# Splitting three rows of a weight load by 117 and 11 partitions, and giving SyncE's load credits once

## The chip, the cores and the metric

The kernel runs on one core of a Trainium2 chip. The metric is the device time of one execution in microseconds (us). Where two kernels are compared by a ratio, it is the mean time of one kernel's fast runs over the mean time of the other's fast runs of the same rounds, so it is not quite the ratio of the medians that are quoted beside it.

## The reference, cut to what matters

One decode step of grouped-query attention for two sequences over a cache of 32,768 positions, times a small gated MLP:

```python
B, Sq, D = 2, 1, 512
Hq, Hkv, Sk, Dh = 32, 8, 32768, 128          # bfloat16
# k_cache, v_cache: [B, Hkv, Sk, Dh]; wo: [Hq * Dh, D]
scores = einsum("bhqd,bhkd->bhqk", q, k) * (Dh ** -0.5)
o = einsum("bhqk,bhkd->bhqd", softmax(scores), v)
s = o.reshape(B, Sq, Hq * Dh) @ wo           # wo comes last
g = silu(mlp(xn))
return x + s * g
```

Nearly all of the work is to read the two caches once: 16 pairs (sequence, head) with 8 MB of K and 8 MB of V each. wo has 4 MB.

## The kernel before

SyncE issues every large load. A K or V load of one pair is one DMA of 128 partitions with 64 KB each; the consumers count its two halves on two semaphores, so SyncE adds 16 to the second semaphore itself. wo is stored as two halves of 128 partitions x 16 rows of 1 KB. It is loaded last, in seven pieces that get smaller, and each piece has a semaphore on which TensorE starts its products.

```python
WO_PARTS = [(0, 0, 8), (0, 8, 16), (1, 0, 8), (1, 8, 12), (1, 12, 14), (1, 14, 15), (1, 15, 16)]

def load(cache, dst, sems, m):
    if m < last:
        sp.dma_start(out=dst, in_=row_view(cache, *groups[m])).then_inc(sems[0], 16)
        sp.sem_inc(sems[1], 16)
    else:
        for c in range(NPART):
            load_half(cache, dst, sems, m, c)
# ...
for m in range(1, NG):
    sp.wait_ge(p_k, m)
    load_k(m)
    sp.wait_ge(p_o, m)
    load_v(m)
wos = A_wo.rearrange("(g p r) d -> p g (r d)", p=128, r=RS)
for i, (g, r0, r1) in enumerate(WO_PARTS):
    w = slice(r0 * D, r1 * D)
    d_wo[i].after(sp.dma_start(out=wo3[:, g, w], in_=wos[:, g, w]), 16)
# ...
def product(i):                              # TensorE
    g, r0, r1 = WO_PARTS[i]
    wait(pe, (d_wo[i], 16))
    # four matmuls for each row
```

The softmax here doesn't subtract the row's maximum and nothing guards it: scores larger than these inputs give would overflow.

## Time and profile before

| | before |
|---|---|
| time, median of 3 runs | 654.95 us (654.88 to 655.34) |
| profiled span | 654.2 us |
| data queue's share of 16 DMA engines | 99.2% |
| first and last of the 16 landings of the last wo load | 649.74, 651.47 us |

From the profile page of the kernel before: the span in 40 slices (DMA in tenths, then GB/s), and the table of DMA queues (packets, MB, share of 16 engines).

```profile
DMA  8999999999999999999999999999999999999997
GB/s 368 442 439 448 442 413 429 445 445 429 417 445 445 441 401 445 445 437 405 445 445 445 409 437 445 445 433 409 445 445 445 397 445 445 445 425 417 437 429 293
...
q1 hardware_dynamic: 6492, 280.50, 99.2%
q8 instruction: 2, 0.03, 0.0%
q14 instruction: 2, 0.02, 0.0%
```

The DMA engines are almost never idle (99.2%), so the kernel is as fast as its loads. What can still differ is the end: the last load is done when the slowest of 16 engines is done. The chain of waits of the kernel before (start, length, what) says the same: one DMA piece up to 651.47 us, then only a few small steps.

```profile
614.34 0.34 SPq L451
614.68 0.05 issue
614.73 36.74 DMA kbuf<-in_A_wo_dram
651.47 0.04 issue
651.52 0.26 PE bank L614 x4
651.78 0.02 issue
651.80 0.30 DVE sg L638
```

The trace's semaphore records give the 16 landings of each load, read here as one for each engine. Of the last wo load:

```
649.74 649.75 649.76 649.77 649.81 649.82 649.83 649.85 649.89 649.99 650.10 650.12 650.22 650.38   650.97   651.47
```

The last two are called the stragglers here. A third engine (650.38) is half a us late.

### The profile page before, as it was taken

Reading aid. Unit: us, or ns where it says so; the run is one execution under the profiler, and the core shown is the slowest. Engines: PE = TensorE matmul, PEld = TensorE weight load, DVE = VectorE, ACT = ScalarE, POOL = GpSimd, SP = SyncE. Lnnn points to the kernel's source line nnn. Section 1 sums busy time; section 2 is a strip of 40 time slices with the busy share of each in tenths; the row PEclk is TensorE's granted clock in tenths of the full one; section 3 lists DMA queues with packets and bytes.
Section 4 is the critical chain, followed back from the end, with each engine's and each line's share of the span. In section 5 each row is a group of like instructions: output and inputs, shape, how many; then the busy total and the mean of one; then the engine's idle time right before and its main releaser. Section 6 shows DMA issues by size and latency. Waiting matters only on the chain. (4 is left out here: it accounts for less than half of the span.)

```text
span 654.2 us, 6541 instructions
## 1 busy us (share of the span) xinstructions
PE 390.2 (60%) x2406; PEld 156.8 (24%) x2438; DVE 345.7 (53%) x412; ACT 76.6 (12%) x184; POOL 7.7 (1%) x29
## 2 busy tenths in 40 slices
PE   0648285582838648293773829367283945828785
PEld 0222132230313212131231213123121322312322
DVE  4257092653909356291844719174480926539570
ACT  1320102010010200101020010201001020010100
POOL 3100000000000000000000000000000000000000
PEclk9769788696978868698786978878697896869798
DMA  8999999999999999999999999999999999999997
GB/s 368 442 439 448 442 413 429 445 445 429 417 445 445 441 401 445 445 437 405 445 445 445 409 437 445 445 433 409 445 445 445 397 445 445 445 425 417 437 429 293
DMA packets 6508, 280.56 MB, mean 429 GB/s; under 512 B 736, under 2 KB 1000, under 8 KB 1256
## 3 DMA queue, kind: packets, MB, share of 16 engines
q1 hardware_dynamic: 6492, 280.50, 99.2%
q8 instruction: 2, 0.03, 0.0%
q14 instruction: 2, 0.02, 0.0%
q10 hardware_dynamic: 12, 0.01, 0.0%
HBM read 280.50 MB, written 0.00 MB: 429 GB/s over the span
## 5 line engine op out<-in xcount | busy, mean ns | idle before, releaser
L562 PE MATMUL bank<-T,z 128*128 128x512 bf16 x992 | 271.6, 418 | 187.2 <-PEq L46 181.7
L489 DVE STREAM_TRANSPOSE T<-kbuf 128x1024 int32<-128x1024 int32 x256 | 290.5, 1206 | 127.2 <-DVEq L46 127.2
L562 PEld LDWEIGHTS bank<-T,z 128*128 128x128 bf16 x1024 | 96.0, 103 | 350.2 <-issue 274.4
L579 PE MATMUL bank<-vbuf,pt 128*16 128x512 bf16 x1024 | 75.6, 461 | 2.5 <-PEq L46 2.5
L466 ACT ACTIVATE ep<-bank 128x512 bf16<-128x512 f32 x32 | 19.1, 597 | 436.1 <-ACTq L46 436.1
L510 DVE RECIPROCAL rec<-bank 128x1 f32<-128x1 f32 (+1 forms) x17 | 2.9, 169 | 122.7 <-DVEq L46 122.7
L579 PEld LDWEIGHTS bank<-vbuf,pt 128*16 128x16 bf16 x1024 | 28.0, 104 | 41.9 <-issue 25.1
L498 DVE STREAM_TRANSPOSE pt<-ep 128x512 bf16<-128x512 bf16 x32 | 22.7, 708 | 22.0 <-DVEq L46 22.0
L544 PE MATMUL bank<-ob,sel_o 128*128 128x128 f32 x136 | 20.6, 298 | 16.4 <-PEq L46 16.4
L572 PE MATMUL bank<-ones_f,sm 128*128 128x1 f32 x32 | 6.6, 277 | 31.3 <-PEq L46 31.3
L544 PEld LDWEIGHTS bank<-ob,sel_o 128*128 128x128 f32 x136 | 17.7, 204 | 21.8 <-issue 21.8
L470 ACT COPY ob<-bank 128x512 f32<-128x512 f32 x16 | 9.4, 586 | 105.7 <-ACTq L46 105.7
L459 ACT ACT_TABLE_LOAD x16 | 20.5, 1283 | 0.3
L572 PEld LDWEIGHTS bank<-ones_f,sm 128*128 128x128 f32 x32 | 5.8, 225 | 32.2 <-issue 32.2
L459 ACT COPY z<-qr 32x16 bf16 x64 | 12.9, 201 | 0.7
L428 PE MATMUL bank<-vbuf,h_bf 128*32 128x512 bf16 x14 | 5.3, 565 | 5.7 <-DVE h_bf L425 5.7
L539 PE MATMUL bank<-ident 128*1 128x1 bf16 x64 | 8.4, 165 | 0.0
L305 PE MATMUL bank<-ident,xn_bf 17*128 17x17 bf16 x4 | 0.3, 179 | 13.4 <-POOL x L296 13.4
L539 PEld LDWEIGHTS bank<-ident 128*1 128x1 bf16 x64 | 4.0, 82 | 16.2 <-issue 14.4
L518 DVE TENSOR_REDUCE oA<-xm 128x128 f32 x16 | 5.9, 366 | 3.8 <-DVEq L46 3.8
L512 DVE SCALAR_TENSOR_TENSOR xm<-bank,rec,mask 128x128 f32<-128x128 f32 (+1 forms) x17 | 6.0, 351 | 2.5 <-DVEq L46 0.2
L466 ACT ACTIVATION_READ_ACCUMULATOR ep<-bank 128x1 f32 x32 | 6.4, 199 | 0.2
(75 smaller groups left out, 55.4 us busy)
## 6 DMA issues: line engine op xcount, KB each, us to landing
vbuf<-in_A_v_cache_dram SPq DMA_DIRECT2D x4, 4096.0 KB, 29.6
kbuf<-in_A_k_cache_dram SPq DMA_DIRECT2D x2, 4096.0 KB, 22.9
kbuf<-in_A_wq_dram SPq DMA_DIRECT2D x1, 4096.0 KB, 12.5
vbuf<-in_B_w_dram SPq DMA_DIRECT2D x2, 1792.0 KB, 17.4
kbuf<-in_A_wo_dram SPq DMA_DIRECT2D x3, 1024.0 KB, 34.4
kbuf<-in_A_wo_dram SPq DMA_DIRECT2D x1, 512.0 KB, 37.1
kbuf<-in_A_wo_dram SPq DMA_DIRECT2D x1, 256.0 KB, 37.3
kbuf<-in_A_wo_dram SPq DMA_DIRECT2D x2, 128.0 KB, 36.8
```

Source lines behind the costliest of these rows:

```text
L459: i = act.copy(out=z[32 * j:32 * j + 32, :, :, c:c + rep], in_=qr[32 * j:32 * j + 32, :, :, bass.ds(m * rep, rep)],)
L466: act.activation(out=eps_[i][:, :], in_=sc[i][:, :], func=ACT.Exp, scale=inv_sqrt_dh, accum_out=rss[i][:, :]).then_inc(s_e, 1)
L470: act.copy(out=ob[:, :], in_=o[:, :]).then_inc(s_ob, 1)
L489: dve.transpose(out=Ts[(NR * i + r) % T_BUFS][:, :].rearrange("p (b t k) -> p t b k", b=NB, t=RT), in_=kt[:, r * W:(r + 1) * W].rearrange( ...
L498: dve.transpose(out=pts[h][:, :, :].rearrange("p r (t h) -> p t r h", h=rep), in_=eps_[i][:, :].rearrange("p (t r h) -> p t r h", r=NR, h= ...
L512: dve.scalar_tensor_tensor(out=xm[p0:, :, :], in0=oT[p0:, :].rearrange("p (w r) -> p w r", w=WL), scalar=rec[p0:, 0:1], in1=mask[p0:, :].u ...
L518: dve.tensor_reduce(out=dst, in_=xm[p0:, :, :].rearrange("p w r -> p r w"), axis=AX.X, op=ALU.add).then_inc(s_r, 1)
L539: pe.matmul(mark_ps, lhsT=ident[:, 0:1], rhs=ident[:, 0:1], start=True, stop=True).then_inc(sem, 1)
L544: mm = pe.matmul(oT, lhsT=sel_o[:, t, :, :, :].rearrange("p j h w -> p (j h w)"), rhs=ob[:, t * Dh:(t + 1) * Dh], start=(t == 0), stop=(t ...
L562: mm = pe.matmul(sc[i][:, :], lhsT=z[:, nb, e, zc:zc + 128], rhs=Tb[:, nb, :, e], start=(r == 0 and nb == 0 and e == 0), stop=(r == NR - 1 ...
L572: pe.matmul(S, lhsT=sms[1][:, :], rhs=ones_f[:, 0:1], start=True, stop=True)
L579: mm = pe.matmul(o[32 * j:32 * j + VT * rep, :], lhsT=pts[h][:, r, a * VT * rep:(a + 1) * VT * rep], rhs=vt[:, u * VT:(u + 1) * VT, :].rea ...
```

## The change

The intent, as the diff suggests: let the high-numbered DMA engines carry less of wo, so that late engines end with the others. Rows 8 to 14 of the second half go as 3 + 3 instead of 4 + 2, and the first three rows are cut at partition 117 into a DMA on 13 engines (117 = 13 x 9) and one on 11. Besides, SyncE's increments for undivided loads are given once at the start.

```diff
-WO_PARTS = [(0, 0, 8), (0, 8, 16), (1, 0, 8), (1, 8, 12), (1, 12, 14), (1, 14, 15), (1, 15, 16)]
+WO_PARTS = [(0, 0, 8, ()), (0, 8, 16, ()), (1, 0, 8, ()), (1, 8, 11, (117,)), (1, 11, 14, ()), (1, 14, 15, ()), (1, 15, 16, ())]
@@ def load
             sp.dma_start(out=dst, in_=row_view(cache, *groups[m])).then_inc(sems[0], 16)
-            sp.sem_inc(sems[1], 16)
@@ after the first load of K
+    sp.sem_inc(s_k[1], 16 * last)
+    sp.sem_inc(s_v[1], 16 * (last - 1))
@@ loads of wo
-        d_wo[i].after(sp.dma_start(out=wo3[:, g, w], in_=wos[:, g, w]), 16)
+        for p0, p1 in zip((0,) + cuts, cuts + (128,)):
+            k_wo = d_wo[i].after(sp.dma_start(out=wo3[p0:p1, g, w], in_=wos[p0:p1, g, w]), 16)
+        l_wo.append(k_wo)
@@ early(i) and product(i): wait for the whole count
-        wait(pe, (d_wo[i], 16))
+        wait(pe, l_wo[i])
```

## The prediction

> **What bounds the kernel.** DMA. The table of DMA queues gives the one data queue 99.2% of 16 engines' span; the 40 slices show DMA at 9 tenths from start to end (280.5 MB, 429 GB/s), PE at 60%, DVE at 53%. The chain of waits ends in one 36.74 us piece, the last wo load (614.73 to 651.47), then 0.26 us of PE, 0.59 us of DVE and the store. So the time is set by when the slowest of the 16 DMA engines finishes its share of the last wo load.

> Every load so far gives every engine the same bytes, but they do not end together. The 16 landings of the last wo load (the trace's semaphore records): fourteen from 649.74 to 650.38, one at 650.97, one at 651.47. The lag is old: the first K load lands within 0.8 us, the next (78.9 us) has two stragglers 1.4 and 1.9 us behind the median, and it persists (1.1 and 1.6) because the queues never drain. In between, at 59.5 and 69.7 us, two 16 KB instruction packets take 0.93 and 0.96 us. [...] I read these as the stragglers' cause.

> **What the change does.** (a) wo rows 8 to 14 of the second half: 4+2 rows become 3+3, the first three loaded by 117 and by 11 partitions. [...] Then engines 13 to 15 carry nothing of those rows. Packets of 1, 2 and 4 KB follow each other after 42, 80 and 155 ns, so 3 KB needs about 118 ns (estimate). Per engine, rows 8 to 14: before 8x155 + 8x80 = 1.88 us; after, engines 0 to 10 18x118 = 2.12 (+0.25), 11 and 12 2.01 (+0.13), 13 to 15 0.94 (-0.94). Total bytes are unchanged. (b) 29 SyncE semaphore increments of 17 ns become two. SyncE waits 528 us for compute before loads while the DMA queue stays fed: 0.0 us. One more DMA issue (about 0.43 us) is off the path too: SyncE ends issuing wo at 622.9, 26 us before those bytes move. PE and DVE programs keep their order.

> **Worth.** If both stragglers are among engines 13 to 15, they end near 650.0 and 650.5, and the next engine (650.38 plus up to 0.25) near 650.6: -0.9 us. If only the slower one is, the other ends at about 651.2: -0.3. If neither: +0.25. I hold the first most likely, since the split was chosen so; the trace doesn't number its engines.

> **Prediction: 654.2 us, range 653.6 to 655.3.** Faster by over 2%: 0.01; within 2%: 0.98; slower: 0.01.

> **What would show it.** Right: the last load's landings span about 0.8 us instead of 1.73 and end near 650.6; the 117- and 11-partition loads show 13 and 11 landings; the first landings come 0.25 us later; both 16 KB instruction packets stay; groups of PE and DVE unchanged; loads issued at the same times. Wrong: a straggler still near 651.2 to 651.7.

> **What would make it wrong.** Stragglers with low numbers; instruction packets moving to other engines or times because SyncE's program is shorter; 3 KB packets costing more than interpolated; chip-to-chip differences as large as the effect.

The sum comes to 654.2 us, 0.75 us of gain between the -0.9 and the -0.3 us under "Worth". Its terms for the engines stand on three counts. The 13 and 11 engines were a supposition then. Equal shares, so 8 or 9 packets for each engine, are an estimate from 128 packets and 16 landings, or 117 and 13. That the engines without cut rows are numbers 13 to 15 was supposed. That the lag persists because the queues never drain is the reading of a data queue at 99.2%, not a separate measurement.

## More of the kernel before

A table by stretches of the kernel before, in us: busy time and instructions of each compute engine, granted clock, DMA share, GB/s. The last column is the one to read.

```profile
644.00:646.00 2.00, 2.00 (x17) 1.02 (x13) 0.00 (x0) 0.59 (x1) 0.00 (x0) 0.50 1.03 434
646.00:648.00 2.00, 1.29 (x14) 0.67 (x13) 0.80 (x3) 0.59 (x1) 0.00 (x0) 0.97 0.98 410
648.00:650.00 2.00, 0.84 (x40) 0.59 (x40) 0.09 (x1) 0.00 (x0) 0.00 (x0) 1.00 0.84 313
650.00:652.00 2.00, 1.16 (x32) 0.53 (x32) 0.20 (x1) 0.00 (x0) 0.00 (x0) 1.00 0.06 23
```

Nearly all engines are busy almost to 650 us (DMA share 0.84 in the last stretch before it); then two finish alone.

## The result

| | before | after |
|---|---|---|
| time, median of 6 runs | 654.96 us (654.88 to 655.34) | 656.31 us (655.87 to 656.47) |
| ratio of fast runs | | 1.0018, 95% interval 1.0005 to 1.0031 |
| profiled span | 654.2 us | 655.1 us |
| landings of the last wo load | 649.74 to 651.47 us | 649.70 to 652.38 us |

The change costs a little more than 1 us, where 0.75 us of gain had been predicted. By the 2% measure it is "same", and no two runs of the two kernels overlap.

The profile page of the kernel after, same lines:

```profile
DMA  9999999999999999999999999999999999999997
GB/s 369 440 440 446 441 432 412 444 444 440 404 444 440 444 436 408 444 444 444 408 436 440 448 436 404 448 440 444 432 412 444 444 440 404 444 440 418 436 428 262
...
q1 hardware_dynamic: 6500, 280.50, 99.2%
q8 instruction: 2, 0.03, 0.0%
...
q14 instruction: 1, 0.01, 0.0%
```

Up to the last slice the level is the same. The bytes and the share are the same too, but the last slice moves 262 GB/s instead of 293. A share of 99.2% doesn't tell an engine whose packet moves at full speed from one whose packet takes longer. (One 8 KB packet of q14, at 617.57 us before, is missing after. It doesn't decide the time: split_only below has it and is slow, uncut lacks it and is not.) The chain of waits of the kernel after:

```profile
611.83 39.93 DMA kbuf<-in_A_wo_dram
651.76 0.04 issue
651.81 0.93 PE bank L618 x19
652.74 0.02 issue
652.76 0.30 DVE sg L642
```

The chain still ends in the wo load. (The piece at L618 is longer only because it is followed back to the load before the last two, which landed at 651.76; the two after it landed at 652.11 and 652.38.) The stretches of the kernel after:

```profile
644.00:646.00 2.00, 1.58 (x22) 0.80 (x15) 0.00 (x0) 0.58 (x1) 0.00 (x0) 0.95 1.02 430
646.00:648.00 2.00, 1.13 (x14) 0.51 (x12) 0.89 (x3) 0.58 (x1) 0.00 (x0) 1.00 1.01 331
648.00:650.00 2.00, 0.30 (x24) 0.33 (x28) 0.00 (x0) 0.00 (x0) 0.00 (x0) 1.00 0.95 238
650.00:652.00 2.00, 1.24 (x56) 0.68 (x44) 0.00 (x0) 0.00 (x0) 0.00 (x0) 0.76 0.30 102
```

Here is the loss: from 646 to 650 us the engines are at least as busy as before (DMA share 1.01 and 0.95, before 0.98 and 0.84), but they move 331 and 238 GB/s where they moved 410 and 313. The records of single packets say which ones are slow (packets from 646.3 us on, durations in ns):

| packets | before | after |
|---|---|---|
| 8 KB | 38, all 309 | 20, mean 388, up to 604 |
| 3 KB | none | 256, mean 171, from 121 to 284 |
| 1 KB | 256, all 46 | 256, mean 58, up to 159 |

The first slow packet of the last stage starts at 646.97 us, about 0.6 us after the first 3 KB packet. Packets of all sizes are slow, the 8 KB ones of an ordinary 128-partition load too: something is shared. The extra time is 256 x (171.3 - 121) + 20 x (387.9 - 309) + 256 x (57.7 - 46) = 17.5 us, over 16 engines 1.1 us each. That is the size of the loss.

The table of DMA issues of the kernel after (KB each, time to landing) shows the two cut loads:

```profile
kbuf<-in_A_wo_dram SPq DMA_DIRECT2D x3, 1024.0 KB, 36.0
kbuf<-in_A_wo_dram SPq DMA_DIRECT2D x1, 384.0 KB, 39.9
kbuf<-in_A_wo_dram SPq DMA_DIRECT2D x1, 351.0 KB
kbuf<-in_A_wo_dram SPq DMA_DIRECT2D x2, 128.0 KB, 39.1
...
kbuf<-in_A_wo_dram SPq DMA_DIRECT2D x1, 33.0 KB
```

Their common semaphore has 26 updates: one at 611.56 and one at 611.96 us, just after each issue, and 24 from 648.66 us on. The 24 are 13 + 11 landings; the first two come 34 us before the first 3 KB packet starts (646.38 us), so they are none. In the load that follows, three engines land early, at 648.93, 649.22 and 649.34 us, the other thirteen from 650.01 on. If the cut load takes the first 13 engines in the numbering that the run labels gives below (supposed), these three are engines 13 to 15, which carried nothing of the cut rows. They lie within 0.4 us of each other, so none of them is a straggler.

### The profile page after: what moved, and what is told of

Read it like the earlier page. It is cut to its first block, busy times and chain, and to the rows that moved or that the text cites. A ratio compares the mean times of both kernels' runs of the same rounds, so it can differ in the third digit from the quotient of the medians.

```text
span 655.1 us, 6515 instructions
## 1 busy us (share of the span) xinstructions
PE 383.7 (59%) x2406; PEld 156.2 (24%) x2438; DVE 346.3 (53%) x412; ACT 76.5 (12%) x184; POOL 7.7 (1%) x29
## 3 DMA queue, kind: packets, MB, share of 16 engines
q1 hardware_dynamic: 6500, 280.50, 99.2%
## 5 line engine op out<-in xcount | busy, mean ns | idle before, releaser
L566 PEld LDWEIGHTS bank<-T,z 128*128 128x128 bf16 x1024 | 98.5, 104 | 353.1 <-issue 274.9
L583 PE MATMUL bank<-vbuf,pt 128*16 128x512 bf16 x1024 | 71.5, 441 | 4.6 <-PEq L46 4.6
L548 PE MATMUL bank<-ob,sel_o 128*128 128x128 f32 x136 | 19.2, 284 | 16.8 <-PEq L46 16.8
L548 PEld LDWEIGHTS bank<-ob,sel_o 128*128 128x128 f32 x136 | 16.5, 191 | 21.8 <-issue 21.8
## 6 DMA issues: line engine op xcount, KB each, us to landing
vbuf<-in_B_w_dram SPq DMA_DIRECT2D x2, 1792.0 KB, 17.4
```

The source lines that it names most:

```text
L548: mm = pe.matmul(oT, lhsT=sel_o[:, t, :, :, :].rearrange("p j h w -> p (j h w)"), rhs=ob[:, t * Dh:(t + 1) * Dh], start=(t == 0), stop=(t ...
L566: mm = pe.matmul(sc[i][:, :], lhsT=z[:, nb, e, zc:zc + 128], rhs=Tb[:, nb, :, e], start=(r == 0 and nb == 0 and e == 0), stop=(r == NR - 1 ...
L583: mm = pe.matmul(o[32 * j:32 * j + VT * rep, :], lhsT=pts[h][:, r, a * VT * rep:(a + 1) * VT * rep], rhs=vt[:, u * VT:(u + 1) * VT, :].rea ...
```

## The experiments

Three theories were set against each other.

- C, collision: the loads by 117 and 11 partitions send several DMA engines to the same part of SBUF at once, and they slow each other and their neighbours.
- P, packets: packets of 3 KB cost more than 1, 2 and 4 KB ones suggest.
- S, SyncE: its shorter program moves load issues or instruction packets.

Theory C rested on a supposed map of partitions to ports. What of it these runs show comes from ports3 below: two engines that write partitions 0 and 1, or 0 and 32, move 25.5 and 28.2 GB/s together; at 0 and 4, or 0 and 64, they move 47.9 and 47.4. Which partitions of a load one engine writes no trace shows; that it takes neighbours (nine of 117) is supposed.

Because profiles of one kernel differ by some tenths of a us in when wo begins, the table below counts from the median landing of the first wo load to the last landing of the last one ("tail").

| run | what differs from before | median us | ratio to before, 95% interval | tail us | 3 KB packets, mean ns |
|---|---|---|---|---|---|
| before (profile above) | | | | 9.10 | none |
| after (profile above) | all | 656.31 | 1.0018 (1.0005 to 1.0031) | 10.34 | 171 |
| credits_only | SyncE's credits | 655.09 | 0.9999 (0.9982 to 1.0015) | 8.85 | none |
| split_only | wo pieces and cut | 656.25 | 1.0017 (1.0000 to 1.0034) | 10.23 | 174 |
| uncut | all, without the cut | 655.22 | 1.0000 (0.9983 to 1.0016) | 9.15 | 121 (every one) |
| cut_126 | cut at 126 | 656.51 | 1.0018 (1.0001 to 1.0035) | 10.43 | 164 |
| cut_121 | cut at 121 | 656.77 | 1.0024 (1.0007 to 1.0041) | 10.51 | 190 |

The first three experiments ran on one chip with the same runs of before (median 655.07), the last two with others (median 655.14).

### credits_only

```diff
     if m < last:
         sp.dma_start(out=dst, in_=row_view(cache, *groups[m])).then_inc(sems[0], 16)
-        sp.sem_inc(sems[1], 16)
...
+    sp.sem_inc(s_k[1], 16 * last)
+    sp.sem_inc(s_v[1], 16 * (last - 1))
```

> Only the semaphore increments of SyncE are changed; wo is loaded as before. Theory C (the loads by 117 and 11 partitions make DMA engines collide): ratio to before 1.000, within 0.0005, about 655.0 us, DMA throughput near 420 GB/s from 647.0 to 648.5 us as before. Theory P (packets of 3 KB cost more): the same 1.000. Theory S (SyncE's shorter program moved instruction packets or load issues): 1.002, about 656.3 us, as the whole change.

655.09 against 655.07 us; every packet of the last stage at full speed (309, 159, 84 and 46 ns for 8, 4, 2 and 1 KB, as before). The credits make no difference that these runs can see, and theory S is out as the cause of the loss.

### split_only

```diff
-WO_PARTS = [... (1, 8, 12), (1, 12, 14), ...]
+WO_PARTS = [... (1, 8, 11, (117,)), (1, 11, 14, ()), ...]
 # with the increments of SyncE left where they were
```

> Only the wo pieces are changed; SyncE increments as before. Theories C and P: 1.002, about 656.3 us, 3 KB packets that take 150 to 280 ns in the last 5 us instead of the 121 ns of the first ones. Theory S: 1.000.

656.25 us: the loads of wo carry the whole loss. 172 of the 256 3 KB packets took over 1.3 times 121 ns.

### uncut

```diff
-(1, 8, 11, (117,)), (1, 11, 14, ())
+(1, 8, 11, ()),     (1, 11, 14, ())
```

> The whole change, but the three rows go in one load of 128 partitions instead of 117 and 11. Theory C: no slow packets, every 3 KB packet near 121 ns, throughput over 400 GB/s until 649 us, ratio 1.000 (0.9995 to 1.0005), about 655.0 us. Theory P: 1.002, slow 3 KB packets stay. Stragglers 1.1 and 1.6 us behind the median at the end, as before.

655.22 us (654.75 to 655.25), and no run overlaps those of split_only (655.88 to 656.59). All 256 packets of 3 KB took exactly 121 ns, so the size of a packet is not the cause and theory P is out. The stretches of the uncut kernel show the speed back:

```profile
646.00:648.00 2.00, 1.24 (x15) 0.62 (x13) 0.86 (x3) 0.58 (x1) 0.00 (x0) 1.00 0.95 389
648.00:650.00 2.00, 1.19 (x52) 0.76 (x52) 0.04 (x1) 0.00 (x0) 0.00 (x0) 1.00 0.69 258
```

(389 is under the 400 that was expected, but the share is lower too: GB/s divided by DMA share is 409 here, 418 before the change and 328 after it. The lower second number is an end that comes earlier: this profile's wo loads run 0.3 us ahead of those of before, and the share is 0.69, not 0.95.)

### cut_126

```diff
-(1, 8, 11, (117,))
+(1, 8, 11, (126,))
```

> The whole change with the cut at 126 [...]. If the 11-partition load, whose packets meet in three groups of partitions, is what costs, ratio 1.0005 or less and 3 KB packets mostly under 150 ns; if the loads of 9 partitions for each engine among loads of 8 collide, 1.001 to 1.002 with packets of 150 to 280 ns, as with 117 and 11.

656.51 us, as slow as the cut at 117. So the loss doesn't need the 11-partition load. What the two cuts share is a load with nine partitions for each engine, followed by a small rest load; the two were not taken apart in the kernel. (Nine for 117 comes from its 13 landings; for 126 it is an estimate by the same division, 14 x 9. How many engines it used is not shown.)

### add_11

The uncut kernel with one more load behind the first three-row piece, to a spare buffer.

```diff
+        if i == 3:
+            sp.dma_start(out=spare[117:128, :], in_=wos[117:128, g, w]).then_inc(s_x11, 16)
```

> The uncut version and, beside it, one more load of 3 KB to partitions 117 to 127 of a spare buffer behind the first three-row load. If those packets collide, the median landing of the last wo load comes 0.4 to 0.6 us later than in the uncut version; if not, 0.14 us later (one packet of 121 ns and its completion). The last landing, engine 12, which carries none of it, should hardly move either way.

Counted from the first wo load, the median landing of the last load came 0.32 us later than in uncut (7.81 against 7.48 us), between the two expectations; 22 of 267 packets took over 1.3 times 121 ns. The last landing didn't move (tail 8.94 us). A few packets are slowed, and it is a minor part.

### labels

The kernel before with sixteen tiny loads behind the thirteenth K load, to number the engines. Engine k-1 is the name given here to the one that lands in the load by k partitions and not in that by k-1 (k up to 16). The trace carries no engine numbers of its own.

```diff
+        if m == 12:
+            for k in range(1, 17):
+                sp.dma_start(
+                    out=lab[0:k, (k - 1) * 32:k * 32], in_=A_wq[0:k, 0:32]
+                ).then_inc(s_lab[k - 1], 16)
...
+    for s in s_lab:
+        sp.wait_ge(s, 16)
```

> The kernel before, with 16 tiny loads (64 bytes for each of 1, 2, ... 16 partitions, each with its own semaphore) behind the K load of the thirteenth group, to number the DMA engines: [...] If both stragglers are engines 13 to 15, the two landings 1.1 and 1.6 us behind appear first in the loads by 14 to 16 partitions; if not, they appear with a smaller k and the number is read off. Time within 0.5% of before, about 656 us (the tiny packets are extra).

The load by k partitions had k landings from the DMA side for every k. An engine that has landed before lands again about 0.18 us later, so the time in load k that continues none of load k-1 is engine k-1's:

```
engine      0      1      2      3      4      5      6      7      8      9     10     11     12     13     14     15
us     504.54    .32    .34 505.34    .20    .39    .66    .33    .40    .30    .26 505.75 506.09    .64    .76  505.03
```

(504 where only the fraction stands; engine 14 may be 504.91.) Check: the 16 landings of the K load in front end with 504.85, 505.11, 505.56 and 505.92 us; 0.19 us added to each of them gives the four latest here within 0.05 us. So in this run the stragglers are engine 12 (latest) and engine 11, and engine 3 is third. It is one look at another program than the changed one; that no straggler is among the three engines without cut rows is seen in the changed kernel, as shown above. The tiny packets cost time of their own (657.19 us).

### cut_121

```diff
-(1, 8, 11, (117,))
+(1, 8, 11, (121,))
```

> The whole change with the cut at 121 [...], so that the two stragglers, which the labels number 11 and 12, are relieved. Without collisions: stragglers 0.97 us earlier, other engines 0.5 us later, 654.4 us, ratio 0.999. With collisions (theory C): slow packets of 150 to 280 ns give back what the stragglers gain: ratio 0.999 to 1.001, and the two last landings no longer stand 1 us behind the rest. If the numbering is wrong, 1.002 or more.

656.77 us, the slowest, and outside of what theory C had allowed it; by the letter of the expectation it speaks against the numbering. It doesn't decide that, because the packets were slowed more than with the cut at 117: 190 ns on average, not 171. By the same division 121 would be 11 engines with eleven partitions each (an estimate, on which the 0.97 us earlier and 0.5 us later rest too; the engines of this load were not counted). Then five engines, 11 to 15, carry nothing of the big cut load; even so the tail is 10.51 us. The last landing, 652.87 us, stands alone 0.8 us behind the next. If five engines are relieved so, the trace speaks for the numbering: in the wo load before the cut rows three engines are late (649.23, 649.87 and 650.21 us, the next at 647.76), in the load after them only one (652.24, the next at 651.49). The other two were thus among the five relieved engines, and since 13 to 15 run ahead, they would be 11 and 12. So relieving two late engines, if that is what happened, did not help while the packets of the others were slowed.

### ports, ports2 and ports3: the collision by itself

Three programs with nothing but loads, each phase waited for. Their outputs are wrong, which doesn't matter for the times.

```diff
+    for step in (1, 4, 20):                               # ports
+        phase(f"seven_{step}", [dst[0:6 * step + 1:step, 0:ROW]], [src(7, ROW, ROW)])
+    for p in (128, 117, 126, 120, 112, 104):
+        phase(f"rows_{p}", [dst[0:p, 0:ROW]], [src(p, ROW, ROW)])
+    loads("q128_117", [[w128], [w117]])                   # ports2: 16 loads of 3 KB rows in turn
+    wide("w0_32", (0, 33, 32))                            # ports3: partitions 0 and 32, 192 KB each
```

> Not the kernel: wrong output on purpose, loads alone, each phase waited for. Seven rows of 64 KB to partitions 1, 4 and 20 apart: one source, one set of seven engines, only the destination differs. If the collision is on the destination side, the 1-apart load (two groups of four partitions) takes about 4 times as long as the 20-apart one (seven groups): about 9.7 us against 2.4 us for the packets; if it is on the memory side or does not exist, all three take 2.4 us. Rows of 64 KB by 128, 117, 126, 120, 112, 104 partitions: theory C expects 128 near 425 GB/s, so 19.6 us, and 117 at 200 to 280 GB/s, 27 to 38 us, although 13 engines alone would give 350 (22 us); theory P expects 117 at 350. Eight short loads of 4 KB, 3 KB, and 3 KB cut 117 and 11: theory C expects 3 KB uncut to have packets near 121 ns and the cut ones about 1.4 times that or more; theory P expects both 3 KB phases alike and slower per byte than 4 KB.

> Wrong output on purpose, loads alone, 16 loads of 3 KB packets in each phase. Theory C, worked out from 121 ns a packet: 128 partitions 8 x 121 ns = 0.97 us a load, 16 us in all. 117 partitions alone, 13 engines of 9 packets: 17.4 us if engines that start together stay out of each other's way (the 64 KB phase suggests it), over 21 us if not. 11 partitions side by side (three groups of four): about 4 packets queue for one group, 0.4 us a load, so 7 us; the same 11 rows to partitions 9 apart: 2 to 4 us. 128 and 117 in turn: 16.5 us without collision, over 20 us with, since engines of both patterns are then at work together. With the 11 added: at least 2 us more. 104 partitions [...]: collides by itself, as in the 64 KB phase, at 170 GB/s, 30 us. Theory P: all patterns near 121 ns a packet.

> Wrong output on purpose, loads alone: 192 KB for each partition from the same rows, only the destination partitions differ. One engine moves 27.1 GB/s (64 KB in 2414 ns). If a port is a set of partitions p to p+3 and p+32 to p+35[...]: partitions 0 and 1 together, and 0 and 32 together, stay near the rate of one port[...]; 0 with 4, and 0 with 64, reach 54; [...] 0, 4, 8, 12 reach 108. Eleven partitions side by side (117 to 127, three ports): [...]limited by the four partitions of one port; 9 apart: near 298 (11 engines). [...]

The grouping by fours in ports, ports2 and cut_126 was supposed when it was written; ports3 shows it as far as its table goes (0 to 3: 27.9 GB/s together; 0, 4, 8, 12: 95.5; 117 to 127: 75.6, three times 25.2).

ports3 is the clearest. From the packet records, bytes over the time from the first packet's start to the last one's end:

| destination partitions | engines | ports, read from the rate | GB/s | 64 KB packet, median ns |
|---|---|---|---|---|
| 0, 1 | 2 | 1 | 25.5 | 5131 |
| 0, 32 | 2 | 1 | 28.2 | 4817 |
| 0, 4 | 2 | 2 | 47.9 | 2420 |
| 0, 64 | 2 | 2 | 47.4 | 2418 |
| 0, 1, 2, 3 | 4 | 1 | 27.9 | 9735 |
| 0, 4, 8, 12 | 4 | 4 | 95.5 | 2420 |
| 117 to 127 | 11 | 3 | 75.6 | 9644 |
| 0, 9, ... 90 | 11 | 11 | 259.7 | 2420 |

```profile
65.00:95.50 30.50, 0.00 (x0) 1.00 0.23 26
96.50:105.50 9.00, 0.00 (x0) 1.00 0.23 87
106.00:136.00 30.00, 0.00 (x0) 1.00 0.63 72
137.00:146.00 9.00, 0.00 (x0) 1.00 0.61 240
```

ports: seven rows of 64 KB took 8.6 us to partitions 1 apart and 3.3 us to partitions 4 or 20 apart, so direction and cause were as expected and the spread packets slower than the 2.4 us written down (2.7 to 3.3). Rows of 64 KB by 128 partitions ran at 408 GB/s, by 117 at 331, by 126 at 350, by 120 at 192, by 112 at 238, by 104 at 168. The expectation that 117 alone would fall to 200 to 280 GB/s was wrong: engines that start together on 117 partitions keep out of each other's way (median packet 2418 ns). On 104 and 120 partitions they do not (5107 ns), nor on 112 (4477 ns). By the division of 117 into 13 x 9 these would be runs of eight on 13 and 15 engines and runs of seven on 16, an estimate: their engines were not counted. Why 117 differs from the three was not shown. In the kernel the loads overlap and engines are up to 1.6 us apart, so they don't start a load together as they do here, where each phase is waited for.

The last phases of ports, eight loads of 3 KB rows, missed their expectation: uncut 10.13 us and a median packet of 121 ns, cut at 117 13.26 us and 135 ns, 1.1 times and not 1.4.

ports2, the same with 3 KB packets; stretches around the phases "128 partitions", "117 partitions" and "128 and 117 in turn":

```profile
3.60:20.90 17.30, 0.00 (x0) 1.00 0.98 364
22.30:43.80 21.50, 0.00 (x0) 1.00 0.76 267
68.20:90.20 22.00, 0.00 (x0) 1.00 0.91 273
```

With short packets 117 partitions alone reach 267 GB/s, under the 331 of long ones; that the engines don't stay in step is a reading. In turn with loads of 128 they took 22.1 us. Without collisions 16.5 us would do (an estimate at 121 ns a packet), and half of each phase alone makes 19.4 us. With the loads of 11 added it took 25.3 us, 3.2 more, where at least 2 more had been expected. These phases show the slowing by mixed loads weaker than the kernel does: packets of 162 ns on average against 131 for 128 alone, in the kernel 171 against 121. The phases with 11 partitions did not tell anything here: 16 loads side by side took 6.2 us and spread ones 12.2 us, the opposite of what was expected. Each load is one short packet for each engine, and the time for each load, 0.39 and 0.76 us, is of the size of an issue (0.43 us in the chain of the kernel before); ports3 put the question again with long packets. The 104 partitions reached 231 GB/s and not 170.

## Why the prediction was wrong, point by point

- **What bounds the kernel: right.** DMA, and at the end the slowest engine's landing. All differences between the versions stand in the tail of the wo loads.
- **How many engines carry what: right.** The cut loads had 13 and 11 landings, and three engines ran ahead (which numbers they have was supposed).
- **SyncE's credits: right.** "0.0 us" was predicted, 655.09 against 655.07 us measured. Both 16 KB instruction packets stayed (52.3 and 69.4 us).
- **"so 3 KB needs about 118 ns (estimate)": the step that failed.** 121 ns is right for a 3 KB packet of the uncut load. The sum then took that time for every engine whatever the others were writing. Cut, the packets took 171 ns on average, and the 8 KB and 1 KB ones beside them were slowed too. The term that had been left out, collision, measures 1.1 us for each engine. For the middle engines the prediction had +0.25 us: 0.25 + 1.1 = 1.35 us, and the median landing of the last wo load moved by 1.39 us (7.50 to 8.89 us after that of the first wo load). The runs with loads alone show that engines that meet at one destination port share the rate of about one engine (25.5 to 28.2 GB/s for two or four of them, 27.1 for one alone). That this is the shared thing inside the kernel too is inferred from its pattern and the uncut run; in the kernel itself it was not separated from a collision on the memory side.
- **"If both stragglers are among engines 13 to 15": failed as well, with as large a share.** The labels number them 12 and 11, and in the changed kernel's trace none is among the three engines that ran ahead (648.93 to 649.34 us). With that alone the sum would have given +0.13 us (the share of engines 11 and 12) instead of -0.9. The gap between 654.2 us predicted and 656.31 us measured is 2.1 us: about 1.0 comes from this step and 1.1 from the collisions. (The 1.1 is an average over 16 engines; the stragglers' own share of it was not measured.)
- **Instruction packets as the stragglers' cause: supported, but their size is not explained.** No run took them away, but one moved. Count the engines over 0.7 us behind the median of a load. In the traces of all kernel versions there is one at the landing at 50.2 us, just after an instruction packet of 8 KB (48.5 to 49.8 us), and there are three at 79.3 us. At 59.9 us there are two in every version whose first 16 KB packet started at 52.2 to 59.7 us, and still one in cut_126, where it started at 62.2 us. And in the two traces that have one more 8 KB packet, at 617.5 us (before and split_only), a fourth engine is late from the next load on (by 0.47 and 0.76 us); uncut, without it, has three. So the late engines come with the packets, one for each, as far as timing can tell. The lags, 0.5 to 1.2 us after an 8 KB packet and 1.3 to 1.9 us after the others, are more than the 0.31 and 0.92 to 0.96 us that the packets take.
- **The idea itself.** In ports3 a port took 25.5 to 28.2 GB/s whether two or four engines wrote it, while one engine alone moves 27.1 GB/s (64 KB in 2414 ns). If a late engine's share of a 128-partition load lies at one port, handing it to other engines can hardly bring those partitions in sooner, even without collisions. This is the author's estimate: that the share lies at one port is not shown, only that 128 partitions ran at 408 GB/s, 16 times 25.5; no version of the kernel without collisions was found to try it on.

No version that beats both kernels came out of this; the uncut one equals the kernel before.

## What to carry to other kernels

In these runs loads by 128 partitions kept their engines out of each other's way (408 GB/s with 64 KB packets), also one after the other (364 with 3 KB packets); loads by 117 and 126 did so only alone and with long packets (331 and 350), loads by 104, 112 and 120 not at all (168, 238 and 192). A partition count chosen for how many engines it uses also decided here how much the engines slowed each other, and that must be measured first. In a DMA-bound kernel, read GB/s by stretches and the durations of single packets, not the DMA share: here it stayed at 1.01 while 331 GB/s moved instead of 410. Balancing 16 engines by bytes presumes that each has a rate of its own; measure the rate in the new pattern before summing packets.
